# Attention and a gated layer on one core: two sorts of GpSimd two units and one unit earlier, and x of units 10 to 15 transposed by DMA

## The chip, the cores and the metric

One core of a Trainium2 chip runs the whole kernel. The core has TensorE (PE, matrix products; PEld is its loading of weights), VectorE (DVE), ScalarE (ACT), GpSimd (POOL) and SyncE (SP). Each takes its own instructions in a fixed order and waits on semaphores for the others. DMAs are issued from the queues of SP, ACT and POOL and run on sixteen shared engines. The metric is the time of one execution on the device in microseconds (us); smaller is better.

## What is computed

The reference, cut to its core. Sliding-window attention with a linear bias comes first (8 batches, 8 heads, 576 positions, 64 per head); its output, as 4608 rows of 512, goes through a gated layer.

```python
scores = scale * np.matmul(q, k.transpose(0, 1, 3, 2))
rel = pos[:, None] - pos[None, :]
bias = slopes[:, None, None] * (-np.abs(rel).astype(np.float32))[None, :, :]
mask = (rel >= 0) & (rel < 128)
scores = np.where(mask, scores + bias[None], -1000000000.0)
attn = softmax(scores)                    # max taken off, sum + 1e-9
x = np.matmul(attn, v)                    # then (batch, position, head * 64)
g = x @ w_gate
silu = g * (1.0 / (1.0 + np.exp(-g)))
out = (silu * (x @ w_val)) @ w_out        # 512 -> 1536 -> 512
```

## The kernel before

**Units and blocks.** Attention is cut into 36 units, nine for each pair of batches: four tiles of 128 positions for either batch and one of both tails of 64. The tile of keys, queries or values that belongs to unit i is called rank i. Units 0 to 8 are batches 0 and 1, units 9 to 17 batches 2 and 3, units 18 to 26 batches 4 and 5. The gated layer works on nine blocks of 512 rows. Block 2 needs the x of units 9 to 12, block 3 that of units 13 to 16; block 8 takes the tails.

**One unit.** `scores` (L341) multiplies transposed keys `kT` with transposed queries `qT` into PSUM (L381, L417), ACT takes the exponential (L387, L421), DVE multiplies with a mask, `weighted` (L429) multiplies with the values on PE (L449), and DVE divides by the sum (L452, L453) into a tile `x`. `x_transposed` (L463) then writes x transposed into the block's tile `xT`. For units below `X_DMA_FROM` = 16 it does so with four transposes on PE (L477, tile `px`) and a copy on DVE or ACT (L479, L481); from unit 16 on SP issues one transposing DMA (L471).

**From memory to kT and qT.** For batches from 2 on a half of a batch (256 positions, all heads) is loaded from POOL's queue (`load_raw`, L224): half (b, g) is half g of batch b. Its two 128-position tiles lie interleaved, so POOL sorts it (`sort`, L280: three copies, L285 to L287, for q and three for k). After that SP issues two transposing DMAs for its two ranks (`by_dma`, L306) into qT and two into kT. Half (2, 0), with ranks 9 and 10, is an exception: PE transposes it (`spread`, L289, tile `pt` at L293) and DVE and ACT copy it out (L296). The tails come through L303. Values (`va`) are loaded by POOL at L237 and L243.

**What sets the order.** POOL's stream is written by hand: first a list of loads (L1048 to L1091), then, at the end of each unit, `loads_at(i)` (L934), which issues the value loads up to rank i + 7, then the sorts that are due, then the loads of halves that are due. A sort is due `SORT_AHEAD` = 6 units ahead of its use, except for the half used at unit 11, which is (2, 1), at unit 7, and the half used at unit 13, which is (3, 0), at unit 8 (`sort_at`, L927). Loads are due 8 units ahead. `attention` (L997) is a generator: after each unit it calls `loads_at(i)`, then `transpose_dma` for the transposes of some units ahead (L1023), then `x_transposed`. From unit `LATE` = 13 on and below `X_DMA_FROM` the x of a unit is kept in a list `waiting` and transposed one unit later. `everything` (L1119) steps through the gated layer (`ffn`, `wide` at L495) and takes steps of attention between its products; the value that the generator yields tells how many units are finished. `transposes_to` (L917) calls `transpose_pe`, which walks the list `pe_order`, with the spreads at its end.

For the first part PE, DVE and ACT have a hand-written order; later on a scheduler in the compiler of the kernel's language places the instructions on PE, DVE, ACT and SP by its own estimates.

Of the kernel before, what the change touches and what calls it, by code (L numbers as in the profile page):

```python
# [15 lines left out]

P = 128
WIN = 128
X_DMA_FROM = 16
AHEAD = 5  # L20
SORT_AHEAD = 6
LOAD_AHEAD = 8
# [37 lines left out]
def kernel(  # L60
# [10 lines left out]
    nc = tc.nc  # L71
# [3 lines left out]
    NKB = DM // P  # L75
# [37 lines left out]
    def later_masks(of):  # L113
        for h in by_slot:
            nc.scalar.activation(reg[:, slot(h), :], of, AF.Exp, scale=-(2.0 ** (-8.0 * (h + 1) / H)))
# [23 lines left out]
    def make_mask(n):  # L139

        if n > 3:
            to = msk[n - 4][:, :, 64 * (n - 4):64 * (n - 4) + 64]
            nc.scalar.copy(runs(to), in_order(reg[:, :, 128:256]))
            return
        to, of = ((msk[0][:, :, 0:64], reg[:, :, 128:192]),
                  (msk[1][:, :, 64:128], reg[:, :, 128:192]),
                  (msk[2][0:64, :, 0:64], reg[0:64, :, 0:64]),
                  (msk[2][64:128, :, 64:128], reg[64:128, :, 64:128]))[n]
        nc.scalar.copy(to, of)
# [34 lines left out]
    last = len(units) - 1  # L184
# [3 lines left out]
    def home(name, rank):  # L188
        return kT[:, (rank + 1) % NK] if name == "k" else qT[:, rank % NQ]
# [59 lines left out]
    def transposed(name, rank):  # L249

        if rank < FIRST:
            pt = ps_f.tile([P, 4, P], FP32 if (name, rank) in hw else FP16, name="pt",
                           tag="gv" if name == "k" or rank == 1 else "po",
                           bufs=3 if name == "k" or rank == 1 else 1)
        else:
            pt = ps_a.tile([P, 4, P], FP16, name="pt", tag="a")
        if (name, rank) in hw:

            for _ in range(IDLE[(name, rank)]):
                nc.tensor.matmul(pt.rearrange("p j t -> p (j t)"), idle[:, 0:P], idle,  # L260
                                 start=True, stop=True)
            for j in range(4):
                nc.tensor.transpose(pt[:, j, :], hw[(name, rank)][:, j * P:(j + 1) * P], idf)
            nc.vector.tensor_copy(home(name, rank), pt)
            return
        t_ = nat_of.pop((name, rank))

        for j in range(4):
            nc.tensor.transpose(pt[:, j, :], t_[:, 2 * j:2 * j + 2, :],
                                idm if rank < FIRST else idm2)  # L270
        if name == "k" and rank >= FIRST:
            nc.scalar.copy(home(name, rank), pt)
        else:
            nc.vector.tensor_copy(home(name, rank), pt)

    def in_pairs(name, half):

        return raw[name, half].rearrange("p h t d -> p (h t d)").rearrange("p (j t c) -> p j t c", j=4, t=RUN)
# [10 lines left out]
    def spread(name, t):  # L289

        pt = ps_a.tile([P, 4, P], FP16, name="pt", tag="a")
        for j in range(4):
            nc.tensor.transpose(pt[:, j, :], in_pairs(name, (2, 0))[:, j, t, :], idm2)  # L293
        w = P // RUN
        to = (kT if name == "k" else qT)[:, 0:RUN, :, w * t:w * t + w]
        (nc.scalar.copy if name == "k" else nc.vector.tensor_copy)(  # L296
            to.rearrange("p c j q -> p j c q"), pt.rearrange("p j (c q) -> p j c q", c=RUN))

    def by_dma(name, rank):

        to, c = home(name, rank), rank % 9
        if c == 8:
            nc.sync.dma_start_transpose(to, nat_of.pop((name, rank)).rearrange("p h d -> p (h d)"))  # L303
            return
        half, r0 = (2 * (rank // 9) + c // 4, c % 4 // 2), P // RUN * (c % 2)
        nc.sync.dma_start_transpose(  # L306
            to.rearrange("p j (t q) -> p (j t) q", t=RUN),
            in_pairs(name, half)[r0:r0 + P // RUN].rearrange("p j t c -> p (j t c)"))
# [6 lines left out]
    raw_order, dma_order, dma_need = [], [], [0] * 9  # L315
# [12 lines left out]
        dma_need.append(len(dma_order))  # L328

    ex = {}  # L330
    scored = [False]
    begun = {}

    def begin_scores(i, q4, par, pool=None, tag="a", bufs=4):
# [121 lines left out]
    xT = {}  # L456
# [6 lines left out]
    def x_transposed(i):  # L463
# [5 lines left out]
        dst = xT[n][:, :, j * P:(j + 1) * P]  # L469
        if i >= X_DMA_FROM:  # L470
            nc.sync.dma_start_transpose(dst, x)  # L471
# [23 lines left out]
    def wide(n, m, which, c1=512):  # L495

        w, ms = wg_sb if which == "g" else wv_sb, slice(m * P, (m + 1) * P)
        ps, c0 = early.pop((n, m, which), (None, 0))
        if ps is None:
            pool, tag, bufs = ((ps_a, "a", 4) if (n, m, which) in OTHER  # L500
                               else (ps_f, "po", 1) if (n, m, which) == (0, 3, "g")
                               else (ps_f, "gv", 3))
            ps = pool.tile([P, 512], FP32, name="p" + which, tag=tag, bufs=bufs)
        for kb in range(NKB):
            nc.tensor.matmul(ps[:, c0:c1], w[:, kb, ms], xT[n][:, kb, c0:c1],  # L505
                             start=(kb == 0 and c0 == 0), stop=(kb == NKB - 1 and c1 == 512),
                             skip_group_check=(n <= 1))
        if c1 < 512:
            early[(n, m, which)] = (ps, c1)
        return ps  # L510
# [393 lines left out]
    def transpose_pe(n):  # L904
        nonlocal done_pe
        while done_pe < n:
            name, rank = pe_order[done_pe]
            (spread(name.lower(), rank) if name.isupper() else transposed(name, rank))
            done_pe += 1

    def transpose_dma(n):
        nonlocal done_dma
        while done_dma < n:
            by_dma(*dma_order[done_dma])
            done_dma += 1

    def transposes_to(i):  # L917
        transpose_pe(pe_need[min(i, 9)])
        transpose_dma(dma_need[min(i, last)])
# [3 lines left out]
    def use_of(which):  # L923
        name, half = which
        return 9 * half + 8 if name == "tail" else first_rank(half[0]) + 2 * half[1]

    def sort_at(which):  # L927
        r0 = use_of(which)
        return {11: 7, 13: 8}.get(r0, r0 - SORT_AHEAD)

    def load_at(which):
        return use_of(which) - LOAD_AHEAD
# [1 line left out]
    def loads_at(i):  # L934
        nonlocal loaded, raws, sorted_
        while loaded <= min(i + 7, last):
            load_v(loaded)
            loaded += 1
        while sorted_ < len(raw_order) and i >= sort_at(raw_order[sorted_]):
            if raw_order[sorted_][0] != "tail":  # L940
                sort(*raw_order[sorted_], nc.gpsimd)
            sorted_ += 1
        while raws < len(raw_order) and i >= load_at(raw_order[raws]):
            if raw_order[raws][0] == "tail":
                load_tail(raw_order[raws][1])
            else:
                load_raw(*raw_order[raws])
            raws += 1

    def run(steps):  # L950
        for fs in steps:
            for f in fs:
                f()
            yield
# [7 lines left out]
    def first_tiles():  # L962

        first_masks()
        transpose_pe(1)
        begin_scores(0, 0, 0)
        transpose_pe(2)
# [29 lines left out]
    def attention():  # L997

        waiting = []
        transposes_to(FIRST)  # L1000
        for _ in run(scores(FIRST)):
            yield FIRST
        for i in range(FIRST, last + 1):
            late = i >= LATE
            if i < last:
                transposes_to(i + 1)
                for n, _ in enumerate(run(scores(i + 1))):
                    yield i - len(waiting)
                    if n == 2 and late:
                        weighted(i)  # L1010
                        yield i - len(waiting)
            if not late or i == last:
                weighted(i)
                yield i
            loads_at(i)
            if i == 4:
                nc.sync.dma_start(dist_s, dist_s_d.ap())
            if i == 7:
                later_masks(dist_s)
            if i == 8:  # L1020
                make_mask(4)
                make_mask(5)
            transpose_dma(dma_need[min(i + (AHEAD if i > 8 else 4 if i > 6 else 3), last)])  # L1023
            yield i - len(waiting)
            if late and i < X_DMA_FROM:
                if waiting:
                    x_transposed(waiting.pop(0))
                waiting.append(i)
                yield i
                yield i  # L1030
                continue
            while waiting:
                x_transposed(waiting.pop(0))
            x_transposed(i)
            yield i
            yield i + 1
# [149 lines left out]
```

## Time and profile before

| what | value |
|---|---|
| median of 3 runs | 342.09 us (342.05 to 342.31) |
| the profiled execution | 342.63 us |
| its span, first to last instruction | 340.9 us |
| software DMA queue (POOL's loads) | 94304 packets, 18.62 MB, 72.5% of 16 engines' span |
| hardware DMA queue 1 (SP) | 45856 packets, 18.76 MB, 35.6% |
| L306, transposing DMAs of q and k | 44 issues, median to landing 5.7 us (qT) and 6.7 us (kT) |
| L471, transposing DMAs of x (units 16 to 35) | 20 issues, to landing 2.4 / 4.5 / 10.6 us (min / median / max) |
| L477, transposes of x on PE | 64, first at 14.2, last at 118.8 us |
| L481, copies of them on ACT | 12, median 0.585 us |
| block 2's first product (L505) | 96.75 us |
| block 3's first product (L505) | 134.84 us |

How to read it: the profile page gives the busy time of each engine and the share of the span; a list of waits says which line of which engine waited for whom, in total, how often and at most; a table by stretches gives busy time, granted TensorE clock (1.00 is full speed) and DMA figures for chosen parts of the span; a timeline lists the instructions of one engine in order of time, merged where they follow each other, with idle time ahead of them and its inferred releaser in brackets. DMA shares over 1 mean that more than one transfer is in hand at an engine on average.

### The profile page before, as it was taken

The numbers are of one execution on the slowest core, as the hardware profiler recorded it, in microseconds if no ns is written. First come the engines' busy times: TensorE is split into PE (matmuls) and PEld (weight loads), VectorE is DVE, ScalarE is ACT, GpSimd is POOL, SyncE is SP. The second block draws the span as 40 slices with busy tenths as digits, with TensorE's granted clock in tenths as the row PEclk, the third lists the DMA queues.
The fourth block names the chain that finished last, engine by engine and source line by source line (L and its number), as shares of the span: only waits on it lengthen the run. The fifth ranks groups of instructions, "written<-read, shape, count | busy, mean of one in ns | idle before, by whom it ended". The sixth has DMA issues, their size and how long they took to land. (4 is left out here: it accounts for less than half of the span.)

```text
span 340.9 us, 7793 instructions
## 1 busy us (share of the span) xinstructions
PE 327.2 (96%) x2931; PEld 217.3 (64%) x2931; DVE 276.8 (81%) x643; ACT 207.4 (61%) x417; POOL 133.3 (39%) x210
## 2 busy tenths in 40 slices
PE   8999998969999999899999999999999999999995
PEld 3664464434456665456665665666688888888884
DVE  4678967959979769998899999999956785775592
ACT  4976688426576566465565646563366776676650
POOL 8967768799469459646409100000000000000000
PEclk9999999979999999999999999999999999999999
DMA  9999999999999999999999944024202112022024
GB/s 153 168 180 176 176 192 161 112 136 183 169 162 106 172 191 123 191 162 139 101 189 156 133 95 92 17 47 62 63 2 64 30 33 64 0 64 51 13 63 123
DMA packets 140885, 38.49 MB, mean 113 GB/s; under 512 B 128560, under 2 KB 136496, under 8 KB 140848
## 3 DMA queue, kind: packets, MB, share of 16 engines
q0 software_dynamic: 94304, 18.62, 72.5%
q1 hardware_dynamic: 45856, 18.76, 35.6%
q10 hardware_dynamic: 688, 0.62, 0.6%
q8 instruction: 23, 0.38, 0.5%
q14 instruction: 14, 0.11, 0.1%
HBM read 37.98 MB, written 9.44 MB: 139 GB/s over the span
## 5 line engine op out<-in xcount | busy, mean ns | idle before, releaser
L505 PE MATMUL pv<-xT,wv_sb 128*128 128x512 f16 (+2 forms) x312 | 77.3, 366 | 0.2
L505 PE MATMUL pg<-xT,wg_sb 128*128 128x512 f16 (+2 forms) x324 | 77.0, 356 | 0.1
L523 ACT ACTIVATE tt<-pg 128x512 f16<-128x512 f32 x68 | 40.9, 603 | 46.3 <-PE pg L505 45.8
L387 ACT ACTIVATE ex<-ps 128x512 f16<-128x512 f32 x96 | 50.2, 606 | 11.4 <-PE ps L381 11.3
L524 DVE SCALAR_TENSOR_TENSOR uu<-tt,pg 128x512 f16<-128x512 f16 x67 | 45.6, 680 | 8.6 <-ACT tt L523 8.3
L535 DVE TENSOR_TENSOR hT<-uu,pv 128x512 f16<-128x512 f16 x68 | 46.1, 679 | 2.1 <-PE pv L505 0.4
L243 POOL DMA_DIRECT2D va<-in_v_dram x56 | 40.3, 749 | 16.6 <-PE av L449 14.4
L505 PEld LDWEIGHTS <-wv_sb 128*128 128x128 f16 x312 | 28.0, 98 | 25.8 <-issue 3.5
L642 PEld LDWEIGHTS <-hT 128*128 128x128 f16 x384 | 37.1, 98 | 11.0 <-DVE hT L596 0.6
L505 PEld LDWEIGHTS <-wg_sb 128*128 128x128 f16 x324 | 28.6, 98 | 23.4 <-issue 2.1
L393 DVE TENSOR_TENSOR ex<-ex,m_reg 128x1024 f16<-128x1024 f16 x42 | 29.0, 696 | 6.6 <-ACT ex L387 6.6
L642 PEld LDWEIGHTS <-S 128*128 128x128 f16 x288 | 27.5, 98 | 8.5 <-issue 2.2
L453 DVE TENSOR_TENSOR x<-av,rec 128x256 f16<-128x256 f32 x72 | 28.4, 418 | 0.4
L642 PE MATMUL po<-T,hT 128*128 128x256 f16 x192 | 26.2, 273 | 0.3 <-DVE hT L596 0.3
L642 PE MATMUL po<-T,S 128*128 128x256 f16 x192 | 25.9, 273 | 0.3 <-ACT u2s L668 0.3
L421 ACT ACTIVATE exc<-psc 128x512 f16<-128x512 f32 x40 | 21.4, 605 | 2.5 <-PE psc L417 2.4
L787 DVE TENSOR_TENSOR hT<-s,v 128x512 f16<-128x512 f16 x18 | 7.6, 423 | 17.7 <-ACT s L786 17.7
L381 PE MATMUL ps<-qT,kT 64*128 64x256 f16 x192 | 16.7, 278 | 4.7 <-DMA qT<-qraw 3.5
L449 PEld LDWEIGHTS <-ex 128*128 128x128 f16 x384 | 17.5, 97 | 4.5 <-issue 1.2
L449 PE MATMUL av<-va,ex 128*128 128x65 f16 x384 | 19.3, 193 | 0.5 <-ACT ex L387 0.3
L381 PEld LDWEIGHTS <-kT 64*128 64x128 f16 x192 | 7.8, 95 | 16.5 <-issue 8.5
L733 PEld LDWEIGHTS <-wg_sb 128*128 128x128 f16 x144 | 14.1, 98 | 1.8
(156 smaller groups left out, 592.2 us busy)
## 6 DMA issues: line engine op xcount, KB each, us to landing
out_dram<-osb SPq DMA_DIRECT2D x50, 128.0 KB, 2.4
va<-in_v_dram POOLq DMA_DIRECT2D x56, 64.0 KB, 7.3
kraw<-in_k_dram POOLq DMA_DIRECT2D x12, 256.0 KB, 7.9
qraw<-in_q_dram POOLq DMA_DIRECT2D x12, 256.0 KB, 6.0
out_dram<-osb SPq DMA_DIRECT2D x8, 256.0 KB, 6.5
wg_sb<-in_moe_w_gate_dram POOLq DMA_DIRECT2D x6, 256.0 KB, 7.7
wo_sb<-in_moe_w_out_dram POOLq DMA_DIRECT2D x3, 512.0 KB, 8.2
wv_sb<-in_moe_w_val_dram POOLq DMA_DIRECT2D x5, 256.0 KB, 8.1
```

What stands on the lines that cost most here:

```text
L243: nc.gpsimd.dma_start(va[rank][n:n + P // run, :, 0:D], src[t])
L381: nc.tensor.matmul(two[par][:, j, :], kT[rows, ks, pair, :], qT[rows, p:p + 2, pair, :], start=(j == 0 and not early_tile), stop=(j == 1))
L387: nc.scalar.activation(e[:, o:o + 2, :], banks[q4][par], AF.Exp, scale=scale)
L393: nc.vector.tensor_mul(e[:, o, :], e[:, o, :], reg[:, o, :])
L421: nc.scalar.activation(er4[:, :, par], banks[par].rearrange("k (a b) q -> k a b q", a=2), AF.Exp, scale=scale)
L449: nc.tensor.matmul(av[:, j, :], w, val, start=(n == 0), stop=(n == len(todo) - 1))
L453: divided[i] = nc.vector.tensor_mul(x[:, 4 * half:4 * half + 4, :], av[:, :, 0:D], rec.broadcast_to([P, 4, D]))
L505: nc.tensor.matmul(ps[:, c0:c1], w[:, kb, ms], xT[n][:, kb, c0:c1], start=(kb == 0 and c0 == 0), stop=(kb == NKB - 1 and c1 == 512), skip_ ...
L523: nc.scalar.activation(tt, pg[:, c0:c1], AF.Tanh, scale=0.5)
L524: nc.vector.scalar_tensor_tensor(out=uu, in0=tt, scalar=one if (n, m) == PIN else 1.0, in1=pg[:, c0:c1], op0=ALU.add, op1=ALU.mult)
L535: product_of[n, m] = nc.vector.tensor_mul(hT[n][:, m, c0:c1], acted[(n, m)][1][:, c0:c1], pv[:, c0:c1])
L642: nc.tensor.matmul(dst, a[:, m, cols], b[:, m, :], start=(start and m == 0), stop=(m == HM - 1), skip_group_check=True)
```

## The change

Three things change. The half (2, 1) is sorted at unit 5 instead of 7, and (3, 0) at unit 7 instead of 8. `X_DMA_FROM` goes from 16 to 10, so the x of units 10 to 15 goes through SP's transposing DMA and the list `waiting` is not used any more. The spreads of half (2, 0) are issued only after the latest wide product that has been recorded, through `tc.issue_after`; and at units 4 to 6 the transposes of four units ahead are asked for instead of three.

```diff
--- before.py
+++ after.py
@@ -16,7 +16,7 @@
 
 P = 128
 WIN = 128
-X_DMA_FROM = 16
+X_DMA_FROM = 10
 AHEAD = 5
 SORT_AHEAD = 6
 LOAD_AHEAD = 8
@@ -328,7 +328,7 @@
         dma_need.append(len(dma_order))
 
     ex = {}
-    scored = [False]
+    scored, last_wide = [False], [None]
     begun = {}
 
     def begin_scores(i, q4, par, pool=None, tag="a", bufs=4):
@@ -502,9 +502,10 @@
                                else (ps_f, "gv", 3))
             ps = pool.tile([P, 512], FP32, name="p" + which, tag=tag, bufs=bufs)
         for kb in range(NKB):
-            nc.tensor.matmul(ps[:, c0:c1], w[:, kb, ms], xT[n][:, kb, c0:c1],
-                             start=(kb == 0 and c0 == 0), stop=(kb == NKB - 1 and c1 == 512),
-                             skip_group_check=(n <= 1))
+            last_wide[0] = nc.tensor.matmul(
+                ps[:, c0:c1], w[:, kb, ms], xT[n][:, kb, c0:c1],
+                start=(kb == 0 and c0 == 0), stop=(kb == NKB - 1 and c1 == 512),
+                skip_group_check=(n <= 1))
         if c1 < 512:
             early[(n, m, which)] = (ps, c1)
         return ps
@@ -905,7 +906,11 @@
         nonlocal done_pe
         while done_pe < n:
             name, rank = pe_order[done_pe]
-            (spread(name.lower(), rank) if name.isupper() else transposed(name, rank))
+            if name.isupper():
+                with tc.issue_after(last_wide[0].ins):
+                    spread(name.lower(), rank)
+            else:
+                transposed(name, rank)
             done_pe += 1
 
     def transpose_dma(n):
@@ -926,7 +931,7 @@
 
     def sort_at(which):
         r0 = use_of(which)
-        return {11: 7, 13: 8}.get(r0, r0 - SORT_AHEAD)
+        return {11: 5, 13: 7}.get(r0, r0 - SORT_AHEAD)
 
     def load_at(which):
         return use_of(which) - LOAD_AHEAD
@@ -1020,7 +1025,7 @@
             if i == 8:
                 make_mask(4)
                 make_mask(5)
-            transpose_dma(dma_need[min(i + (AHEAD if i > 8 else 4 if i > 6 else 3), last)])
+            transpose_dma(dma_need[min(i + (AHEAD if i > 8 else 4), last)])
             yield i - len(waiting)
             if late and i < X_DMA_FROM:
                 if waiting:
```

In POOL's stream the six copies that sort half (2, 1) move from behind the loads of half (3, 0) and four value loads to ahead of them; those of half (3, 0) move from behind the loads of half (3, 1) and two value loads to ahead of these loads. All else on POOL keeps its place.

SP's instructions stand in this order in the two built programs, from the transposes of half (4, 0) to the x of unit 16 (stores of results left out; numbers are ranks, or units for x; where a half's two ranks come together their order is not told):

```
before:  q18 q19  k18 k19            q20 q21  k20 k21      q22 q23  k22 k23  x16
after:   q18 q19  x10  k18 k19  x11 x12  q20 q21  k20 k21  x13  q22 q23  k22  x14  k23  x15  x16
```

PE loses 24 transposes and 24 loads of weights. Its first wide product of block 2 waits for the DMAs of x10, x11 and x12 in the changed program. The sixteen spread transposes stand together behind six wide products (four matmuls each) that followed them before; of the L562 matmuls 19 instead of 10 stand between the x of unit 7 and the scores of unit 10.

## The prediction

> All times are on the axis of the profiled execution of before, whose span is 340.9 us of 342.63 us. The runs shown have a median of 342.09, 0.54 below it; I add a difference worked out in the profile to that median.
>
> **What bounds the kernel now.** First the page's busy times, then the list of TensorE's (PE's) waits (total, times, longest).
>
> ```profile
> PE 327.2 (96%) x2931; PEld 217.3 (64%) x2931; DVE 276.8 (81%) x643; ACT 207.4 (61%) x417; POOL 133.3 (39%) x210
> ```
>
> ```profile
> PE ps L381 <- DMA qT<-qraw: 3.5, 1, 3.5
> ...
> PE pt L293 <- POOL qraw L286: 0.9, 1, 0.9
> ```
>
> PE is the bound: its waits are one of 3.5 us, one of 0.9 and scraps. A late PE start of a block goes to the end nearly one for one: from 96.75 to 336.7 PE is busy 238.1 of 240.0 us. Next the busy times by stretch around the 3.5 us wait (columns: length, busy PE, PEld, DVE, ACT, POOL, then granted clock, DMA, GB/s).
>
> ```profile
> 67.32:70.81 3.49, 0.01 (x2) 0.01 (x2) 1.82 (x4) 0.70 (x2) 3.33 (x6) 1.00 1.25 95
> 70.81:74.24 3.43, 3.43 (x14) 1.31 (x15) 1.27 (x2) 2.06 (x4) 3.12 (x7) 0.50 1.58 156
> 74.24:80.00 5.76, 5.76 (x43) 2.85 (x41) 5.57 (x13) 2.07 (x4) 5.34 (x11) 1.00 1.78 169
> ```
>
> After the wait PE runs 3.43 us at clock 0.50: 1.72 us lost on top of 3.48. Then the timelines of PE, POOL and SP (start, duration, work) where block 2 of the second layer begins.
>
> ```profile
> 93.73 0.28 PE L477 MATMUL px<-idm,x 128*128 128x128 f16 x2
> ...
> 94.71 0.28 PE L477 MATMUL px<-idm,x 128*128 128x128 f16 x2
> ...
> 96.75 1.04 PE L505 MATMUL pg<-xT,wg_sb 128*128 128x512 f16 x4
> ```
>
> ```profile
> 79.05 1.36 POOL L222 DMA_DIRECT2D small<-in_k_dram  x2
> 80.38 1.39 POOL L222 DMA_DIRECT2D small<-in_q_dram  x2
> 81.72 1.41 POOL L237 DMA_DIRECT2D va<-in_v_dram  x2
> 83.05 0.96 POOL L230 DMA_DIRECT2D qraw<-in_q_dram  x1
> 83.93 0.96 POOL L230 DMA_DIRECT2D kraw<-in_k_dram  x1
> 84.80 2.81 POOL L243 DMA_DIRECT2D va<-in_v_dram  x4
> 90.30 0.40 POOL L285 COPY aside<-qraw 128x256 f16<-128x256 f16 x1 [2.69 <-DMA qraw<-in_q_dram]
> ...
> 94.38 0.40 POOL L285 COPY aside<-kraw 128x256 f16<-128x256 f16 x1 [2.75 <-DMA kraw<-in_k_dram]
> ```
>
> ```profile
> 91.65 2.51 SPq L306 DMA_TRANSPOSE qT<-qraw  x2
> 95.73 2.52 SPq L306 DMA_TRANSPOSE kT<-kraw  x2
> ```
>
> Unit 12's x is transposed on PE at 93.73 to 94.71, 2 us before block 2's first matmul (96.75) reads it. SP meanwhile issues transposes for units 18 and 19, far from needed; but each pair waits for POOL's sort of half (4,0), at 91.65 and 95.73.
>
> **The change, part by part.** *The sort of half (2,1) from unit 7 to 5.* In POOL's stream it moves ahead of the loads of (3,0) and of four v loads. Its loads, issued at 49.14 and 50.56, took 9.9 and 10.6 us; POOL's own counter waits put their ends at 59.31 and 61.73. So it sorts q at 59.3 to 60.7 and k at 61.7 to 63.2 (1.4 us for three copies), where before it began at 65.29. The first transpose goes out at 60.7, not 66.69, and lands 4.5 us later, at 65.2. PE comes to unit 10's scores at 67.3 + 1.9 (nine L562 matmuls more stand ahead of them, at 0.216) - 0.9 (next paragraph) = 68.3. The 3.48 us wait and its 1.72 us of slow clock go.
>
> *Spreads after the latest wide matmul.* The wait on POOL L286 (0.86 us) goes; unit 9's scores now follow the spread copies more closely, a cost between nothing and those 0.86 us. Neither end reaches the result: PE arrives early at block 2 either way (below).
>
> *The price, on POOL.* Loads and sorts ran apart; now each sort stands soon behind its own load and POOL waits. The six loads of q from 59 to 116 us landed after 5.5, 4.9, 7.1, 5.9, 5.9 and 6.4 (median 5.9), those of k after 5.8, 7.1, 10.3, 6.9, 7.1 and 7.8 (7.1). From 63.2: load q and k of (3,0) 0.9 each, four v loads 2.7, to 67.7; q has landed at 63.2 + 5.9 = 69.1, sorted 70.5; k at 64.1 + 7.1 = 71.2, sorted 72.6. Half (3,1): issued 72.6 and 73.5, q sorted at 79.9, k landed at 80.6, sorted 82.0. The tails (2.7) and two v loads (1.3) bring POOL to 86.0, where before it loaded (4,0) at 83.05. That q lands at 91.9 and is sorted at 93.3, its k (86.9 + 7.1) at 95.4: 1.7 us later than before for q.
>
> *x of units 10 to 15 by SP.* Off PE go 24 transposes; a pair of them put between other matmuls moved these by 0.11 us (88.01 to 88.12), so 0.65 us for units 10 to 12 and 0.65 for 13 to 15. ACT loses six copies of 0.585 us, and was not the bound. On come six DMA transposes in SP's queue. In the changed program SP's order there is: q 18, q 19, **x 10**, k 18, k 19, **x 11, x 12**. So x of unit 12, needed at once, stands behind four transposes needed at unit 17 or later, whose first waits for the sort of (4,0). PE's first matmul of block 2 waits for all three x transfers; behind it on PE stands everything else.
>
> An issue takes 1.31 us from start to start (91.65, two of them, to 94.16 with the gaps). x 12 is seventh: 93.3 + 6 x 1.31 = 101.2. For issue to landing I take the first four x transfers of before, which ran beside loads like these (5.8, 5.6, 7.4, 5.5; median 5.7); all twenty go from 2.4 to 10.6. It lands at 106.9. SP's reuse of each of eight completion counters adds nothing: eight issues are 10.5 us, longer than all but that 10.6.
>
> PE gets to block 2 at 96.75 - 3.48 - 1.72 - 0.86 - 0.65 = 90.0 and waits 16.9 us: what the early sort gained is spent in the new wait. Block 2 starts 106.9 - 96.75 = 10.15 us later than before, then runs cold as after the shorter wait (+1.72), and 12 fewer transposes follow (-0.65). Sum +11.2 us: span 352.1, profiled time 353.8, and against the median 353.3.
>
> *Units 13 to 15.* Block 3 started at 134.84, unit 16's x, already by DMA, was issued at 120.69 and landed at 126.5: 8 us of cover. The four x of block 3 move with PE, and the sorts that SP waits for before them (5,0) move less; cost nothing. If that cover went, PE would wait again by what it overruns.
>
> *Bounds.* If POOL kept before's times (91.63 and 95.70), x 12 would be issued at 99.6, and with the fastest landing (2.4) block 2 starts at 102.0: +6.3, 348.4. If POOL waited for no load at all after 63.2, its work alone (19.1 us) puts the q load at 82.3, and with the fastest figures (4.9, then 2.4) x 12 lands at 98.9: 345.3, still slower. Upwards: q 7.1, k 7.8 and 10.3 as in the late rows, x 7.4 give k sorted at 100.0, x 12 issued at 104, landed at 111.4: +15.7, 357.8.
>
> The Trainium skill, page "DMA: Bandwidth & Descriptors", section "Issuing engines are not separate DMA queues", calls a sequencer's time to initiate a DMA usually small beside the DMA itself; here the rows have 1.31 us against 5.7, and six issues ahead make 7.9, more than the transfer. By the rule alone, with x 12 going out when ready, the wait would vanish and the time be that of the first rival. The page "VectorE: DVE Perf Modes", section "Rules for kernel authors", speaks against the change: transpose 128x128 on TensorE where PSUM will do, xbar DMA otherwise. Its table under "The three transpose paths" has 1309 ns for the DMA of one 128x128 block; taken for a whole x it would land x 12 at 102.5 and give 348.9, an estimate from that page. The rows of before (2.4 at least) decide.
>
> **Rivals.** *In time: faster.* If SP is free when x 12 is ready, at 87.7 (before: 94.49, the end of the second multiplication of L453, less PE's lead of 6.7), it lands at 93.4: block 2 starts 3.35 earlier than before, cold (+1.72), and 0.65 follows: -2.3, 339.8; landing in 2.4, with no cold clock, it is 335.0. For it: x 12 is ready well ahead of 96.75. Against: its place in SP's order, and the sorts ahead, whose lowest bound is 345.3. It decides from an issue by 90.0 on (90.0 + 5.7 = 95.7, where the gains and the cold clock balance). Chance 0.04.
>
> *Short wait.* POOL loses nothing and the transfers find emptier DMA engines: 345.3 to 348. For it: POOL idles more, so fewer loads are in flight. Against: hardware and software queues were busy in all slices to 200 us. Chance 0.10.
>
> *A second wait.* The (5,0) transposes stand ahead of x 14 to 16; if POOL falls back a further 8 us, block 3 waits too: 358 to 365. Against: 8 us of cover, and POOL gains on PE while PE waits. Chance 0.05.
>
> *The sort does not help:* unit 10 still waits for qT. It would cost nothing more, because PE waits at block 2 anyway: within the forecast.
>
> **How the numbers follow.** Forecast 0.80, 353.3, its range 348 to 357.5; the short wait 0.10, the second wait 0.05, in time 0.04, a chance meeting at no change 0.01. The range 348 to 357.5 leaves out 0.20. A measurement tells 0.2% (0.7 us) from no change: faster 0.04, same 0.01, slower 0.95.
>
> **What would show it.** Right: the 3.5 us wait on qT gone; a PE wait of 12 to 20 us at L505 on the DMA of xT that ends between 102 and 111; clock 0.5 for about 3.4 us behind it; SP's L471 issues directly behind L306 issues that follow POOL L287. Wrong: SP with x 12 out before 95, or block 2 starting before 98.

## The result

| | before | after |
|---|---|---|
| median of 4 runs | 342.07 us (342.01 to 342.31) | 359.1 us (357.5 to 361.73) |
| the profiled execution | 342.63 us | 357.83 us |
| its span | 340.9 us | 356.1 us |
| mean granted TensorE clock | 0.994 | 0.970 |
| block 2's first product | 96.75 us | 110.55 us |

The ratio after to before is 1.0505, 95% interval 1.0443 to 1.0566: slower by 17.0 us where 11.2 were forecast, 1.6 us above the range. (Ratios leave out runs in a slower state, four of e1's ten and the profiled one of e5, 668.2 us; medians, but for e5's, are of all runs.) First the page of the kernel after: busy times, then the span in 40 slices (PE and the granted clock).

```profile
PE 328.0 (92%) x2907; PEld 217.1 (61%) x2907; DVE 276.2 (78%) x643; ACT 204.6 (57%) x411; POOL 135.7 (38%) x210
...
PE   8999999999305999999999999999999999999995
...
PEclk9999999999855999999999999999999999999999
```

PE's busy time hardly moved (327.2 to 328.0 us) and its share fell from 96% to 92%: the loss is idle time in one place, the hole at slices 11 to 13, with a slow clock behind it. The list of PE's waits of the kernel after (total, times, longest):

```profile
PE pg L505 <- DMA xT<-x: 18.2, 1, 18.2
PE nil L172 <- DVE kT L122: 1.2, 1, 1.2
PE po L563 <- DMA wo_sb<-in_moe_w_out_dram: 0.8, 1, 0.8
```

The 3.5 us wait for qT and the 0.9 us wait for the sorted qraw are gone; one wait of 18.2 us stands in their place, and a new one of 0.8 us, for the output weights. The timeline of PE, then that of SP in the kernel after (start, duration, work, idle time before):

```profile
91.74 0.61 PE L381 MATMUL ps<-qT,kT 64*128 64x256 f16 x8
110.55 1.87 PE L505 MATMUL pg<-xT,wg_sb 128*128 128x512 f16 x4 [18.21 <-DMA xT<-x]
```

```profile
95.35 2.51 SPq L306 DMA_TRANSPOSE qT<-qraw  x2
97.96 1.21 SPq L471 DMA_TRANSPOSE xT<-x  x1
99.28 2.90 SPq L306 DMA_TRANSPOSE kT<-kraw  x2
102.27 2.71 SPq L471 DMA_TRANSPOSE xT<-x  x2
```

PE is ready for block 2 at 92.34. SP issues nothing from 93.1 to 95.35, when POOL has sorted q of half (4, 0); then q 18, q 19, x 10, k 18, k 19, x 11 and x 12 follow, 1.2 to 1.6 us each. The last goes out at 103.69 and lands 6.7 us later, at 110.42. POOL's timeline of the kernel after says why q is sorted only then:

```profile
86.79 0.96 POOL L230 DMA_DIRECT2D qraw<-in_q_dram  x1
...
93.84 0.56 POOL L285 COPY aside<-qraw 128x256 f16<-128x256 f16 x1 [1.66 <-DMA qraw<-in_q_dram]
...
94.93 0.40 POOL L287 COPY qraw<-aside 128x256 f16<-128x256 f16 x1
```

The load is issued at 86.79 (83.05 before) and takes 6.9 us. Last, the stretches of the kernel after around the wait (length, busy PE, PEld, DVE, ACT, POOL, then granted clock, DMA, GB/s):

```profile
92.34:95.67 3.33, 0.01 (x2) 0.00 (x0) 1.71 (x3) 1.89 (x4) 1.37 (x3) 1.00 1.78 169
95.67:110.55 14.88, 0.00 (x0) 0.03 (x1) 0.00 (x0) 0.00 (x0) 10.73 (x19) 0.50 1.63 169
110.55:116.15 5.60, 5.60 (x24) 2.75 (x25) 3.20 (x8) 0.86 (x2) 3.59 (x6) 0.50 1.55 180
116.15:120.00 3.85, 3.85 (x41) 2.24 (x40) 2.41 (x5) 2.67 (x6) 2.32 (x5) 1.00 2.21 124
```

The clock falls to 0.50 while PE waits, at 95.67, and stays there until 116.15: of PE's first 5.60 us of work half, 2.80 us, is lost. The sum in spans: block 2 starts 13.80 us later (110.55 - 96.75); from there to the end it is 245.55 us against 244.15, 1.40 more (2.80 of clock, less 1.40 that the missing transposes and scraps give back). Together 15.20, the difference of the two spans. The remaining 1.8 of the 17.0 us come from where the profiled executions lie: that of after is 1.27 below its median, that of before 0.56 above its own.

### The profile page after: what moved, and what is told of

Same layout as the page of the kernel before. It is cut to its first block, busy times and chain, and to the rows that moved or that the text cites. A ratio compares the mean times of both kernels' runs of the same rounds, so it can differ in the third digit from the quotient of the medians.

```text
span 356.1 us, 7757 instructions
## 1 busy us (share of the span) xinstructions
PE 328.0 (92%) x2907; PEld 217.1 (61%) x2907; DVE 276.2 (78%) x643; ACT 204.6 (57%) x411; POOL 135.7 (38%) x210
## 5 line engine op out<-in xcount | busy, mean ns | idle before, releaser
L505 PE MATMUL pg<-xT,wg_sb 128*128 128x512 f16 (+2 forms) x324 | 78.2, 359 | 18.3 <-DMA xT<-x 18.2
L505 PE MATMUL pv<-xT,wv_sb 128*128 128x512 f16 (+2 forms) x312 | 78.0, 366 | 0.1
L505 PEld LDWEIGHTS <-wg_sb 128*128 128x128 f16 x324 | 29.2, 99 | 43.4 <-issue 21.2
L505 PEld LDWEIGHTS <-wv_sb 128*128 128x128 f16 x312 | 28.1, 98 | 25.8 <-issue 4.2
L452 DVE RECIPROCAL rec<-av 128x4 f32<-128x4 f32 x72 | 10.1, 165 | 18.9 <-PE av L449 18.8
```

The lines of the kernel that those rows point to most:

```text
L505: last_wide[0] = nc.tensor.matmul(ps[:, c0:c1], w[:, kb, ms], xT[n][:, kb, c0:c1], start=(kb == 0 and c0 == 0), stop=(kb == NKB - 1 and c1 ...
```

## The experiments

Eight kernels have a time. Each ratio is against runs of the kernel before on the same chip, whose medians there were 342.26 us (340.37 to 344.47, beside e1 to e4) and 342.06 us (340.66 to 344.61, beside e5 to e8). My theory was that x 12's place in SP's queue, behind transposes that wait for POOL's sort, is the loss (Q); the rivals were that the earlier sorts cost it on POOL, or that the transfers of x themselves are too slow.

**e1: the change without x by DMA.** Both sorts early, the spreads as in after, x of units 10 to 15 on PE.

```diff
-X_DMA_FROM = 10
+X_DMA_FROM = 16
```

> Early sorts and the held-back spreads of the changed kernel, but x of units 10 to 15 on PE as before. Theory Q (the loss is x of unit 12 standing in SP's queue behind transposes that wait for the sort of half (4,0)): no wait at block 2; the gains that the changed kernel had before block 2 stay, 3.48 us wait and 1.72 us slow clock gone: 335.5 to 338 us. Rival S (the early sorts themselves cost, because POOL loads and sorts half (4,0) 3.7 us later): slower than before, over 343 us.

Measured: 342.72 us (338.62 to 346.47, 10 runs), ratio 0.997 (0.9927 to 1.0014; the quotient of the medians is 1.001, no gain either). The loss is gone, so it belongs to the move of x; rival S, over 343 us, is not borne out. But the gain that I had counted on is missing too. PE's waits in e1, then its timeline at block 3 and the stretch behind it:

```profile
PE pg L505 <- DMA xT<-x: 2.7, 1, 2.7
PE po L563 <- DMA wo_sb<-in_moe_w_out_dram: 1.5, 1, 1.5
...
PE px L477 <- DVE x L453: 0.9, 1, 0.9
```

```profile
134.17 1.28 PE L505 MATMUL pg<-xT,wg_sb 128*128 128x512 f16 x4 [2.66 <-DMA xT<-x]
```

```profile
134.82:138.23 3.41, 3.41 (x12) 1.65 (x11) 2.05 (x4) 0.60 (x1) 3.15 (x5) 0.50 2.15 150
```

Block 2 begins at 93.25, 3.5 us earlier than before; block 3, where PE did not wait before, now waits 2.7 us for x by DMA and then loses 1.7 us of clock (half of 3.41). SP's timeline in e1 has the pattern of the main loss a second time, 30 us later:

```profile
120.85 2.60 SPq L306 DMA_TRANSPOSE kT<-kraw  x2
123.54 1.28 SPq L555 DMA_DIRECT2D out_dram<-osb  x2
124.92 3.95 SPq L471 DMA_TRANSPOSE xT<-x  x2
```

x 16 (the first of the two) is issued 4.2 us later than before (120.69), because k of half (5, 0) ahead of it is sorted only at 120.8 (115.5 before). POOL, which now stands waiting behind its loads, is later while PE is earlier.

**e2: k 18 and k 19 behind x 12.** The kernel after, with SP's order q 18, q 19, x 10, x 11, x 12, k 18, k 19.

```diff
-            by_dma(*dma_order[done_dma])
+            name, rank = dma_order[done_dma]
+            with tc.issue_after(x_dma[12].ins) if name == "k" and 17 < rank < 20 else ExitStack():
+                by_dma(name, rank)
```

> The changed kernel with SP's order q18 q19 x10 x11 x12 k18 k19: two of the four transposes ahead of x12 moved behind it. Theory Q: x12 issued after q sorted plus four issues instead of six, 2 x 1.35 us earlier, and no wait for the sort of k: block 2 starts 3 us earlier, 355 to 357 us. Rival L (the wait is the transfer's own latency beside loads, not its place in the queue): no change, 358 to 361.

Measured: 357.41 us (354.56 to 358.04, 4 runs), ratio 1.0427 (1.0362 to 1.0493). Below after's, but the intervals overlap, and it is inconclusive as a step: the profiled execution still waits 18.0 us. Two issues fewer stood ahead of x 12, but the sort of q ended at 96.9 in that execution (one copy of POOL's, at 79.83, took 2.61 us in place of some 0.4), and x 12, issued at 102.19, landed after 8.1 us where it took 6.7 in after. Moving only what stands behind the sort of q leaves the sort itself ahead.

**e3: x 10 to 12 ahead of everything that waits.** All three x go out before the tails' transposes and before those of ranks 18 and later.

```diff
-            by_dma(*dma_order[done_dma])
+            name, rank = dma_order[done_dma]
+            if rank == 17 and 12 not in x_dma:
+                return
+            with tc.issue_after(x_dma[12].ins) if 16 < rank < 27 and 12 in x_dma else ExitStack():
+                by_dma(name, rank)
```

> The changed kernel with x10, x11 and x12 ahead of the tails' transposes and of all of ranks 18 on in SP's queue. Theory Q: x12 issued when ready, at 89.3 us on the changed kernel's axis, landed after 5 to 7 us, block 2 at 94.5 to 96.5 instead of 110.55: 15 us less, about 343.5, 341 to 346 us. Rival L: block 2 still waits 15 us or more, over 355.

Measured: 347.63 us (347.11 to 350.81, 4 runs), ratio 1.018 (1.0101 to 1.0259). Two thirds of the loss go with the order in one queue alone; the size was missed. SP's timeline, PE's, and the stretch behind the wait in e3:

```profile
89.53 4.95 SPq L472 DMA_TRANSPOSE xT<-x  x3
```

```profile
101.59 1.87 PE L506 MATMUL pg<-xT,wg_sb 128*128 128x512 f16 x4 [8.64 <-DMA xT<-x]
```

```profile
101.59:105.02 3.43, 3.43 (x16) 1.51 (x17) 1.27 (x5) 0.60 (x1) 3.03 (x6) 0.50 1.06 159
```

x 12 is issued at 93.14, ten us earlier than in after. What is left is the path itself: x 10, 11 and 12 landed after 7.9, 9.4 and 8.3 us, and the loads that POOL had issued from 88 on took 10.1 to 12.9. PE was there at 92.95, just before x 12 was out.

**e4: the sorts as before, x by DMA.** The kernel before with `X_DMA_FROM` = 10; the transposes of ranks from 20 on are held behind x 12, so that ranks 18 and 19 alone can stand ahead of it.

```diff
-X_DMA_FROM = 16
+X_DMA_FROM = 10
...
-            by_dma(*dma_order[done_dma])
+            name, rank = dma_order[done_dma]
+            with tc.issue_after(x_dma[12].ins) if 19 < rank < 27 else ExitStack():
+                by_dma(name, rank)
```

> The kernel before with only x of units 10 to 15 moved to SP (sort times as before), SP's order q18 q19 k18 k19 x10 x11 x12, then q20 on. Theory Q: sorts of (4,0) end near 91.6 and 95.7, x12 is issued at about 100.8 and lands near 107.5: block 2 is 10.7 us late plus 2 us of cold clock, minus 1.3: 352 to 355 us, with the 3.5 us wait on qT still there. Rival S (the sorts' move is the greater part of the loss): under 348.

Measured: 355.85 us (353.81 to 358.39, 4 runs), ratio 1.0401 (1.0326 to 1.0477). PE's waits, and SP's timeline in e4:

```profile
PE pg L506 <- DMA xT<-x: 14.0, 1, 14.0
PE ps L382 <- DMA qT<-qraw: 3.1, 1, 3.1
```

```profile
91.89 4.19 SPq L306 DMA_TRANSPOSE qT<-qraw  x2
96.72 2.51 SPq L306 DMA_TRANSPOSE kT<-kraw  x2
99.33 4.21 SPq L472 DMA_TRANSPOSE xT<-x  x3
```

With POOL at its old pace and the qT wait still there, block 2 starts at 110.03, half a microsecond from after. (The time is just above the expected range; x 12 went out at 102.25, not 100.8, and landed at 109.89.) The move of x by itself makes 13.6 us of loss where after has 17.0, and the two intervals overlap; the early sorts and the spreads bring PE to the same wait sooner, and it waits the longer.

**e5 to e8: where the sorts' gain goes.** e1 had left a question that the prediction answered wrongly: if the qT wait goes, why is the kernel not faster? e5 is e1 with (3, 0) sorted at its old time; e6 is e5 with x of units 13 to 15 by DMA; e7 is the kernel before with (2, 1) alone sorted at unit 5, e8 with it sorted at unit 6.

```diff
 # e5, from e1
-        return {11: 5, 13: 7}.get(r0, r0 - SORT_AHEAD)
+        return {11: 5, 13: 8}.get(r0, r0 - SORT_AHEAD)
 # e6, from e5
-X_DMA_FROM = 16
+X_DMA_FROM = 13
 # e7, from before (e8: 11: 6)
-        return {11: 7, 13: 8}.get(r0, r0 - SORT_AHEAD)
+        return {11: 5, 13: 8}.get(r0, r0 - SORT_AHEAD)
```

> As the first experiment (x of units 10 to 15 on PE, spreads held back), but only half (2,1) is sorted early, at unit 5; half (3,0) stays at unit 8 as before, so POOL issues the loads of (3,1) before it waits for those of (3,0). Theory F (the first experiment gained 3.5 us at block 2 and gave it back at block 3 because POOL fell back 3 to 5 us by sorting (3,0) early): sorts of (4,0) and (5,0) end within 1.5 us of before, no wait at block 3, 336.5 to 340 us. Rival D (block 3 waits for x of unit 16 whenever PE comes early): 341.5 to 343.5, block 3 still waits 2 us or more.

> The fifth experiment with x of units 13 to 15 also by SP's transposing DMA, ahead of x16 in the same queue. Theory Q (place in SP's queue): x16 is issued 3 to 5 us later than in the fifth experiment and block 3 waits, 2 to 6 us slower than it. Rival P (12 transposes less on PE are worth their 0.65 us): 0.5 us faster to no change.

> The kernel before with one edit: half (2,1) sorted at unit 5 instead of 7. Theory F: the 3.5 us wait on qT and its 1.7 us of slow clock go, the 0.9 us wait on the spread stays, POOL does not fall back: 336.5 to 339.5 us. Rival D: the gain is lost at block 3, 341 to 343.

> The kernel before with half (2,1) sorted at unit 6 instead of 7, behind the loads of (3,0) and two value loads. Theory F: sorted from about 64 us, first transpose at 65.4, landed near 70: the wait on qT shrinks to 2 to 3 us, 339.5 to 341.5. Rival D: no change, 341.5 to 343.

| | median, us | ratio to before | block 2's / block 3's first product | PE's wait for xT by DMA |
|---|---|---|---|---|
| before | 342.07 | | 96.75 / 134.84 | none |
| e1 | 342.72 | 0.997 (0.9927 to 1.0014) | 93.25 / 134.17 | 2.7 |
| e5 | 344.96 (three runs) | 1.0104 (1.0071 to 1.0137) | not read | not read |
| e6 | 348.74 | 1.0197 (1.0148 to 1.0247) | 93.71 / 137.03 | 2.6 in two waits, 2.2 at block 3 |
| e7 | 344.11 | 1.0067 (1.0044 to 1.009) | 92.82 / 134.94 | 3.9 |
| e8 | 343.26 | 1.0026 (0.9987 to 1.0064) | 93.38 / 134.26 | 2.6 |

e5 has no trace to read its waits from. e6 is 3.8 us above e5, within what the queue theory gave; its x 16 goes out at 129.72, against 124.92 in e1 (e5's can't be read). In e8 the wait for qT shrank further than expected, to 0.3 us, and the time did not follow. e5, e6 and e7 are slower than before beyond their intervals; e1 and e8 can't be told from it. Why e5 is slower than e1, where (3, 0) too is sorted early, no trace here shows. The faster kernel that I expected of e5 and e7 is not there. PE's timeline in e7 at block 3, then SP's:

```profile
134.94 1.64 PE L505 MATMUL pg<-xT,wg_sb 128*128 128x512 f16 x4 [3.87 <-DMA xT<-x]
```

```profile
121.72 2.58 SPq L306 DMA_TRANSPOSE kT<-kraw  x2
124.40 1.10 SPq L554 DMA_DIRECT2D out_dram<-osb  x2
125.59 3.76 SPq L471 DMA_TRANSPOSE xT<-x  x2
```

Whether (2, 1) is sorted at unit 5 or 6, alone or with (3, 0), block 2 comes 3.0 to 3.9 us sooner. In e1, e7 and e8 block 3 then starts where it did before (134.17 to 134.94 against 134.84), but after a wait for x 16. The slow clock is not gone either: before has 3.41 us at 0.50 behind its qT wait, and e1, e7 and e8 each have 3.41 us at 0.50 behind block 3's start.

In before x 16 landed at 126.53, 8.3 us ahead of PE. Three things use that up. In e1 PE comes 3.3 us earlier (131.51), x 16 goes out 4.2 us later, and its transfer takes 3.4 us longer; the traces of before and of e1 have for that one issue:

```profile
DMA to landing us min/median/max: 5.8/5.8/5.8
```

```profile
DMA to landing us min/median/max: 9.2/9.2/9.2
```

The same three are 3.8, 4.9 and 3.5 us in e7 and 3.2, 3.2 and 4.5 us in e8. So the later issue is not enough by itself: with before's 5.8 us x 16 would have landed at 130.8, 131.4 and 129.8 in the three, and PE would have waited 0.4 us at most (an estimate from these rows). In all three, as in before, x 16 follows the transposes of half (5, 0) in SP's queue. Whether the early sorts would gain if it did not stays open: four more kernels, e1, e7 and before with x 16 ahead of these transposes and e1 with x 16 on PE, were written down with their expectations, and none has a measured time. No version that beats the kernel before was found.

## Why the prediction was right in kind and wrong in size

**Right: the mechanism.** x 12 stood behind q 18, q 19, x 10, k 18, k 19 and x 11, the first of them waiting for POOL's sort of (4, 0), and PE waited at block 2's first L505: 18.2 us, predicted 16.9 and, as a sign, 12 to 20 ending by 111. e3 shows the queue's order to be most of it, e1 that there is no loss without x's move, e4 that the move alone makes 13.6 of the 17.0 us. The rival in time fell: x 12 was not out before 95. So did the short wait (345.3 to 348) and the second wait, since block 3 did not wait in after; that 359.1 lies among the times given to the second wait (358 to 365) is luck, and comes of the larger first wait.

**Right: the early sort removes the qT wait, and the spread wait goes.** Both are gone.

**Wrong: the sum of the path to x 12's landing.** The step "it lands at 106.9" is 3.65 us short of block 2's actual start, 110.55. Its terms:

| term | predicted | after |
|---|---|---|
| load of q of (4, 0) issued | 86.0 | 86.79 |
| q sorted | 93.3 | 95.33 |
| x 12 issued (six issues later) | 101.2 (7.9) | 103.69 (8.36) |
| x 12, issue to landing | 5.7 | 6.7 |
| block 2 starts | 106.9 | 110.55 |

The sort gives 2.0 us: 0.8 from POOL's issue, 1.0 from a load of 6.9 in place of the median 5.9, and 0.2 in the copies. The issues give 0.5, the landing 1.0, and 0.1 passes from the last landing to PE. The choice that failed was the middle of before's rows for each transfer. The row of before for this very load of q had 7.1 us; x 10 to 12 took 6.7 to 7.9 us in after, 7.6 to 7.9 in e4 and 7.9 to 9.4 in e3. The upper ends that I had named (7.1 and 7.4) were the better values. That the row of seven transposes makes the transfers slow is likely and not shown: in that same row q 18 and q 19 landed after 4.6 and 3.8 us.

**Wrong: the clock behind the wait.** "Then runs cold as after the shorter wait (+1.72)": it was 2.80, 5.60 us at 0.50. The step took the length of one slow stretch for that of any; what sets it is worked out in the last section.

**Wrong, without effect on the time: PE's arrival.** "PE gets to block 2 at 90.0" was 92.34. In e1, where x is still on PE, the same gains should have brought PE there at 90.7 (96.75 less 3.48, 1.72 and 0.86) and it came at 93.25: of the 2.6 us that are missing 1.5 went into a wait for the output weights that did not exist before, and 0.5 into a longer one for x (0.9 us, 0.4 before); the other half microsecond is not accounted for. In after this only shortened the wait.

**Wrong: one profile for the median.** In spans the sum was 4.0 us short (15.20 against 11.2): 3.65 of path and 1.08 of clock, less 0.75 that PE gave back beyond the forecast. With this alone the time would have been 342.09 + 15.2 = 357.3, still inside the range. What took it out is the step "I add a difference worked out in the profile to that median", which puts the spread of the runs at nothing: the four runs of after lie between 357.5 and 361.73, the profiled one near the low end, and those of before within 0.3. That is the other 1.8 us. (The upper bound worked out there, 357.8, lay past the range's end of 357.5 too.) Why the runs of after differ is not shown, as one of them was traced.

**Not foreseen: what the sorts are worth alone.** The prediction let the sorts' gain be "spent in the new wait"; I took it for real otherwise, and so my expectations of e1, e5 and e7 had 335.5 to 340 us. They measured 342.72, 344.96 and 344.11.

The page "DMA: Bandwidth & Descriptors" of the Trainium skill (section "Issuing engines are not separate DMA queues") calls the time to start a DMA usually small beside the DMA. For one it was about a fifth here (1.2 to 1.6 us against 6.7 for x 12), but the six between q's sort and x 12 add up to 8.36 us, more than the transfer. The rule on the page "VectorE: DVE Perf Modes", section "Rules for kernel authors", that 128x128 transposes belong on TensorE where PSUM will do, agrees with e1 against after, 342.72 against 359.1 us, though what e1 saves is a place in a queue.

## What to carry to other kernels

Before a transfer is given to an in-order queue, read what stands ahead of it there and what each of those waits for: four transposes that no unit needed yet, and a sort that they waited for, held the x that was needed at once, and the x put first won back two thirds of the loss. When a wait is removed, look for the next block's last arrival, by how much it was ahead, and what the change does to its issue and to its transfer: 8.3 us of lead were used up here. For a transfer that an engine will wait for, take the row of the profile that lies nearest in time, or the slow rows, not the median, and leave room for runs that differ from the profiled one.

## What the runs showed of the hardware that was not expected

**The clock changes in steps of 3.41 us.** Tables by stretches, cut finely, give the times between which the granted clock was 0.50 (us; the last column is the part of them behind PE's restart):

| | PE idle | clock at 0.50 | its length | behind the restart |
|---|---|---|---|---|
| before | 67.32 to 70.81 | 70.82 to 74.23 | 3.41 | 3.41 |
| e1 | 131.51 to 134.17 | 134.82 to 138.23 | 3.41 | 3.41 |
| e3 | 92.95 to 101.59 | 98.21 to 105.04 | 6.83 | 3.45 |
| e4 | 96.06 to 110.03 | 101.33 to 114.99 | 13.66 | 4.96 |
| after | 92.34 to 110.55 | 95.67 to 116.15 | 20.48 | 5.60 |

The lengths are 1, 1, 2, 4 and 6 times 3.41 us. Count such steps from where the clock fell: after restarts at 110.55 in the step from 109.32 to 112.74, and full clock comes at the end of the next one, 116.15. The other rows fit as well: the clock returns at the end of a step that PE worked through. So, by these rows, the slow stretch does not go by how long PE idled but by where in a step it starts again, between 3.4 and 6.8 us once the clock has fallen (an estimate from them). The Trainium skill's page "TensorE: Matmul & The Clock Gate" (section "Part 1: The HAM clock gate") has a free-running window of about 3.4 us and full clock after at least one busy window; the steps of 3.41 us agree.

**Loads beside three transposes of x were slow.** In e3 q and k of (4, 0) took 10.1 and 11.5 us from issue to landing; in the other kernels whose trace can be read q took 6.6 to 8.2 us and k 8.0 to 11.3. That the transposes slow the loads is not shown: the 11.3 us are e4's, where no transfer of x was in hand then.

**The runs of after spread more than those of before.** They lie in 357.5 to 361.73 us, beside 342.01 to 342.31. Beside the experiments before itself spread over 340.37 to 344.47, so that the transfer on the path is the reason is not shown.
